# Attention-stage projections as 256-column groups that share one PSUM bank

## The chip, the cores and the metric

The kernel runs on one core of a Trainium2 chip. The metric is the device time of one launch in microseconds. All times below are of that kind or come from one profiled execution of the kernel before.

## The reference

A transformer layer with pre-LayerNorm: attention with 32 heads over a sliding window of 256 positions, and then a feed-forward network with SiLU, each with its residual. Inputs are bf16.

```python
B, S, D = 1, 2048, 1024;  H = 32; Dh = 32; W = 256;  F = 3584
qkv = _layernorm(x) @ wqkv                    # q, k, v per head
scores = einsum("bhqd,bhkd->bhqk", q, k) * Dh**-0.5
mask = (i - j >= 0) & (i - j < W)
o = softmax(where(mask, scores, -1e9)) @ v
h = x + o.reshape(B, S, D) @ wo
h2 = h + silu(_layernorm(h) @ w1) @ w2
```

## The kernel before

The 2,048 tokens are four blocks of 512 (`NB` = 4), and the model dimension is eight tiles of 128 (`KT` = 8). The order of instructions on every engine is the order of the code (the tile framework's manual schedule); the framework adds the semaphore waits that the accesses call for.

The projections are built from groups: eight matmuls of 128x128 weights with 512 moving columns, accumulated in one bank of PSUM, then one copy by VectorE (`dve`) into SBUF. `v_group` (L235 to L242) makes 128 tokens by 512 columns of v, `qk_group` (L244 to L252) makes 128 columns of q or k for the 512 tokens of a block, and `wo_group` (L266 to L276) makes 128 tokens by 512 columns of the output projection, which VectorE adds to the residual (L273) and a late DMA stores to `h_dram`. The bank comes from `next_acc` (L231), which goes through `acc_banks` in turn; in the attention stages these are the two banks `acc0` and `acc1`. [...]these two, two for attention's outputs (`o_ps`), and four for scores (`sc`).

There are four attention stages, each of 24 groups. In stages one to three the dense work is the v, q and k projection of blocks 1, 2 and 3, and in stage four the output projection of blocks 0 to 2. Woven into each is the attention of the block before. An object `Stream` (L415) holds this as a list of bursts (the score matmuls of four or eight heads, followed by exponentials on ScalarE and by masks on GpSimd) and a list of pieces (the products of the probabilities with v in `attn_out`, L377, and for each 8 of them a reciprocal and a multiplication on VectorE, `attn_norm`, L392). Before each matmul of a group, `between(kt)` is called, 192 times a stage. By two conditions on its count (L435 and L438) it issues a burst or a piece so that they are spread evenly; the first stage has 16 of each and the others 20. TensorE's instructions thus stand as: a few dense matmuls, a burst or a piece, a few dense matmuls, and so on.

After each group the stage takes one step from a list `steps`: the LayerNorm of a later block, on VectorE. A statistics step (`ln_stats`, L176) has two `bn_stats` of 512 columns and one aggregation; four further steps find the reciprocal root (`rstd_steps`, L184), and four scale a tile (`ln_norm`, L201). When the steps are done, `turns` issue DMA transposes. In stage three (block 3) no steps are left; in stage four they are the second LayerNorm of block 0, taken from n = 12 on, two for each group from n = 16.

Work on VectorE is done in program order, so a copy out of PSUM stands behind the steps and attention norms issued before it. Before the four stages lie the projections of block 0, and after them the feed-forward network, with six banks in `acc_banks`; those use `v_group`, `qk_group` and `wo_group` as they are.

Of the kernel before, what the change touches and what calls it, by code (L numbers as in the profile page):

```python
# [9 lines left out]
F32 = mybir.dt.float32  # L10
I32 = mybir.dt.int32
ACT = mybir.ActivationFunctionType
ALU = mybir.AluOpType

P = 128
# [29 lines left out]
def kernel(  # L45
# [10 lines left out]
    nc = tc.nc  # L56
# [3 lines left out]
    S, D = x2d.shape  # L60
    F = B_w1.shape[1]
    H = N_HEADS
    DH = D // H
    assert DH == 32 and D == 1024 and S == 2048 and F == 3584
    KT = D // P
    FT = F // P
    NB = S // 512
    G = H // 4
# [4 lines left out]
    small = ctx.enter_context(tc.tile_pool(name="small", bufs=2))  # L73
# [5 lines left out]
    h_dram = dram.tile([S, D], BF16, name="h_dram")  # L79
# [26 lines left out]
    wqk = view(r_w, 0, KT, 2 * D)  # L106
    wv = view(r_w, 16384, KT, D)
    w1 = view(r_w, 0, KT, F)
    lnT_b = [view(r_w, 24576, KT, 512), view(r_t, 0, KT, 512)]
    x_ring = [view(r_o, i * 1024, 1024) for i in range(8)]  # L110
    wo = view(r_o, 0, KT, D)
    t_in = [view(r_t, i * 1024, 1024) for i in range(2)]
    r_in = [view(r_a, 16384, 1024), view(r_a, 17408, 1024), *t_in, view(r_a, 22528, 1024), view(r_a, 23552, 1024)]
    t_out = [view(r_t, 2048 + i * 1024, 1024) for i in range(2)]
    qT = [view(r_a, (4096, 8192, 12288, 0)[b], G, 512) for b in range(NB)]
    kT = [view(r_a, 16384 + 4096 * b, G, 512) for b in range(NB)]
    v = view(r_a, 32768, S // P, H, VW)
# [55 lines left out]
    def ln_half(xt, stats, c):  # L173
        nc.vector.bn_stats(out=stats[:, c, :], in_=xt[:, c * 512:(c + 1) * 512])

    def ln_stats(xt, st, j, half_done=None):  # L176
        stats = half_done
        if stats is None:
            stats = small.tile([P, 2, 6], F32, name="ln_st", tag="ln_st")
            ln_half(xt, stats, 0)  # L180
        ln_half(xt, stats, 1)
        nc.vector.bn_aggr(out=st[:, j, :], in_=stats[:])
# [46 lines left out]
    acc_banks = list(a[:] for a in acc_ps)  # L229

    def next_acc():  # L231
        acc_n[0] += 1
        return acc_banks[acc_n[0] % len(acc_banks)]

    def v_group(b, j, c, copy, between=None):  # L235
        acc = next_acc()
        for kt in range(KT):
            if between:
                between(kt)
            nc.tensor.matmul(acc, lhsT=lnT_b[b % 2][:, kt, j * P:(j + 1) * P], rhs=wv[:, kt, c * 512:(c + 1) * 512],  # L240
                             start=(kt == 0), stop=(kt == KT - 1))
        copy(out=v[:, b * 4 + j, c * 16:(c + 1) * 16, 0:DH], in_=acc.rearrange("p (h d) -> p h d", d=DH))  # L242

    def qk_group(b, which, g, copy, between=None):  # L244
        acc = next_acc()
        col0 = which * D + g * P
        for kt in range(KT):
            if between:
                between(kt)
            nc.tensor.matmul(acc, lhsT=wqk[:, kt, col0:col0 + P], rhs=lnT_b[b % 2][:, kt, :],  # L250
                             start=(kt == 0), stop=(kt == KT - 1))
        copy(out=(qT, kT)[which][b][:, g, :], in_=acc)  # L252
# [7 lines left out]
    late = []  # L260

    def run_late():
        while late:
            late.pop(0)()

    def wo_group(b, j, c, between=None):  # L266
        acc = next_acc()
        for g in range(G):
            if between:
                between(g)  # L270
            nc.tensor.matmul(acc, lhsT=qT[b][:, g, j * P:(j + 1) * P], rhs=wo[:, g, c * 512:(c + 1) * 512],  # L271
                             start=(g == 0), stop=(g == G - 1))
        nc.vector.tensor_tensor(out=t_out[j % 2][:, c * 512:(c + 1) * 512], in0=acc,  # L273
                                in1=r_in[(b * 4 + j) % 6][:, c * 512:(c + 1) * 512], op=ALU.add)
        if c == 1:
            late.append(lambda: nc.sync.dma_start(out=h_dram[(b * 4 + j) * P:(b * 4 + j + 1) * P, :], in_=t_out[j % 2]))  # L276
# [138 lines left out]
    class Stream:  # L415
# [18 lines left out]
        def between(self, kt):  # L434
            if self.seen * self.n >= self.done * 192:  # L435
                self.bursts[self.done]()
                self.done += 1
            if self.seen * self.n * 2 >= (self.given * 2 + 1) * 192:  # L438
                if pending:
                    pending.pop(0)()  # L440
                coming.append(self.pieces[self.given])
                if len(coming) > self.behind:
                    pending.append(coming.pop(0))
                self.given += 1
            self.seen += 1

    dve, act = nc.vector.tensor_copy, nc.scalar.copy


    st, rs = ln_tiles("a")  # L450
# [99 lines left out]
    for j in range(4):  # L550
        load_x(1, j)

    def ln1_steps(b):
        st, rs = ln_tiles("a")
        xs = [x_ring[(b % 2) * 4 + j] for j in range(4)]
        steps = [lambda j=j: ln_stats(xs[j], st, j) for j in range(4)]
        steps += rstd_steps(st, rs)
        for j in range(4):
            steps.append(lambda j=j: ln_norm(xs[j], st, rs, j))
        return steps, [lambda j=j: ln_transpose(xs[j], lnT_b[b % 2], j) for j in range(4)]  # L560

    def ln2_steps(b):
        st, rs = ln_tiles("b")
        hb = h_blk[b]
        load = lambda: nc.sync.dma_start(out=hb, in_=h_dram[b * 512:(b + 1) * 512, :].rearrange("(j p) d -> p j d", p=P))
        steps = [load]
        steps += [lambda j=j: ln_stats(hb[:, j, :], st, j) for j in range(4)]
        steps += rstd_steps(st, rs)
        for j in range(4):
            steps.append(lambda j=j: ln_norm(hb[:, j, :], st, rs, j))  # L570
        turns = [lambda j=j: ln_transpose(hb[:, j, :], ln2T[b], j) for j in range(4)]
        return steps[:-2] + [turns[0], steps[-2], turns[1], steps[-1]] + turns[2:]

    steps = sum(ln1_steps(1), [])
    for g0 in range(0, G, 4):
        for w in range(2):
            for g in range(g0, g0 + 4):
                qk_group(0, w, g, dve if g % 2 else act)
                n = g0 * 2 + w * 4 + g % 4
# [5 lines left out]
    def load_w1(kt):  # L585
        nc.sync.dma_start(out=w1[:, kt, :], in_=w1_v[:, kt, :])
# [4 lines left out]
    steps, turns = ln1_steps(2)  # L591
    pending, coming = [], []
    stream = Stream(0)
    dense = [lambda j=j, c=c: v_group(1, j, c, dve, stream.between) for j in range(4) for c in range(2)]
    dense += [lambda w=w, g=g: qk_group(1, w, g, dve, stream.between) for g in range(G) for w in range(2)]
    for n in range(24):
        run_late()
        dense[n]()
        if steps and n >= 1 and n != 3:
            steps.pop(0)()  # L600
        elif turns and n % 3 == 2:
            turns.pop(0)()
# [2 lines left out]

    for b in range(2, NB):
        stream = Stream(b - 1)
        dense = [lambda j=j, c=c: v_group(b, j, c, dve, stream.between) for j in range(4) for c in range(2)]
        dense += [lambda w=w, g=g: qk_group(b, w, g, dve, stream.between) for g in range(G) for w in range(2)]
        if b + 1 < NB:  # L610
            for j in range(4):
                load_x(b + 1, j)
            steps, turns = ln1_steps(b + 1)
        else:
            steps, turns = [], []
            nc.sync.dma_start(out=wo[:, 0:4, :], in_=wo_v[:, 0:4, :])
            nc.sync.dma_start(out=wo[:, 4:8, :], in_=wo_v[:, 4:8, :])
            load_res(0)
            load_res(1)
        for n in range(24):  # L620
            run_late()
            if b == NB - 1 and n in (4, 10, 14):
                load_w1({4: 7, 10: 6, 14: 5}[n])
            dense[n]()
            if steps and n >= 1 and n != 3:
                steps.pop(0)()
            elif turns and n % 3 == 2:
                turns.pop(0)()
        assert not steps and not turns


    dense = []
# [6 lines left out]
    steps = []  # L639
    stream = Stream(NB - 1)  # L640
    for n in range(24):
        run_late()
        if n % 2 == 0 and n >= 2 and n // 2 + 5 < S // P:
            load_res(n // 2 + 5)
        wo_group(*dense[n], stream.between)
        if n in (1, 4, 7, 12, 15):
            load_w1((1, 4, 7, 12, 15).index(n))
        if n == 9:
            steps = ln2_steps(0)
            steps.pop(0)()  # L650
        if n == 17:
            nc.sync.dma_start(out=w2[0], in_=w2_v[:, 0:4, :])
        for _ in range(1 if n < 16 else 2):
            if steps and n >= 12:
                steps.pop(0)()
# [29 lines left out]
    for b in range(NB):  # L685
# [4 lines left out]
        for ft in range(FT):  # L690
            acc = h1_group(b, ft)
# [7 lines left out]
            if b == 0 and 6 <= ft < 14:  # L699
                j, c = divmod(ft - 6, 2)  # L700
# [4 lines left out]
        steps = ln2_steps(b + 1) if b + 1 < NB else []  # L705
# [5 lines left out]
        for j in range(4):  # L711
# [9 lines left out]
            for acc, (c0, c1) in zip(accs, cols):  # L721
                mm2(acc, j, c0, c1, early, FT)
                nc.vector.scalar_tensor_tensor(out=t_out[j % 2][:, c0:c1], in0=acc[:, 0:c1 - c0], scalar=0.5,  # L723
                                               in1=t_in[j % 2][:, c0:c1], op0=ALU.mult, op1=ALU.add)
# [36 lines left out]
```

## Time and profile before

| what | value |
|---|---|
| time, median of 3 runs | 691.38 us (691.37 to 691.72) |
| the profiled execution, its own time | 691.51 us |
| its span, first to last instruction | 689.8 us |
| granted TensorE clock, mean | 1.000 |
| start and projections of block 0 | 0 to 49.4 us |
| the four attention stages | 49.4 to 285.2 us |
| the feed-forward network | 285.2 to 689.8 us |
| HBM | 70 GB/s over the span |

The page gives, for each engine, the time in which it was busy and its share of the span; the chain that ended last is followed back from the last instruction to what released each. PE stands for TensorE's matmuls, PEld for its weight loads, DVE for VectorE, ACT for ScalarE and POOL for GpSimd. A group line has the source line, the engine, the operation, the names written and read, shapes and count, then busy time, mean length in ns, and the engine's idle time just before these instructions with what ended it. Matmuls are pipelined: a 512-column matmul is shown with 379 ns while the next one starts 216 ns after it. Some matmul records are missing from the trace, a few in a hundred.

### The profile page before, as it was taken

The page shows a single profiled execution, that of the slowest core. Times are in us where ns is not written, and L with a number is a line of the kernel's source. Part 1 is how long each engine was busy: PE and PEld are TensorE (multiplying, and loading weights), DVE is VectorE, ACT ScalarE, POOL GpSimd, SP SyncE. Part 2 cuts the span into 40 slices and gives each one's busy share as a digit, 9 for nine tenths or more (in the row PEclk, how much of TensorE's full clock was granted, in tenths as well). Part 3 has the DMA queues.
Part 4 walks back from the last instruction along what each step waited for, and adds up shares of the span by engine and source line. Part 5 has one row for each costly group of instructions (what it writes and reads, how often), then busy time and mean ns, then how long its engine had stood idle before and what let it go on. Part 6 is the DMA issues. An engine that isn't in the chain of part 4 may idle for free.

```text
span 689.8 us, 14125 instructions
## 1 busy us (share of the span) xinstructions
PE 676.4 (98%) x5895; PEld 331.6 (48%) x6011; DVE 290.0 (42%) x613; ACT 244.7 (35%) x464; POOL 160.6 (23%) x295
## 2 busy tenths in 40 slices
PE   9999999999999999999999999999999999999998
PEld 4444555555555555544444444444444444444445
DVE  5267646744444449534316133343133251333111
ACT  7326666676666667421310033300133100233000
POOL 1007666566666656500000000000000000000000
PEclk9999999999999999999999999999999999999999
DMA  7842342136341889871023310022200023100110
GB/s 258 275 63 70 48 97 38 25 63 184 73 131 18 251 226 298 207 267 60 2 85 114 85 39 0 1 91 70 85 0 1 27 88 92 38 1 1 30 39 24
DMA packets 78640, 61.48 MB, mean 89 GB/s; under 512 B 52464, under 2 KB 62704, under 8 KB 78576
## 3 DMA queue, kind: packets, MB, share of 16 engines
q1 hardware_dynamic: 77888, 59.78, 31.0%
q8 instruction: 47, 0.77, 0.5%
q10 hardware_dynamic: 688, 0.79, 0.3%
q14 instruction: 17, 0.14, 0.1%
HBM read 39.85 MB, written 8.39 MB: 70 GB/s over the span
## 4 chain that ended last, share of the span: by engine, by line
PE 97%; issue 1%; DMA 0%; DVE 0%; DVEq 0%
PE hacc L671 19%; PE hacc L708 17%; PE acc L250 16%; PE acc L708 10%; PE acc L671 9%; PE acc L240 7%; PE acc L271 7%; PE o_ps L383 5%; PE sc L303 3%; PE hacc L271 1%; PE sc L355 1%; PE o_ps L240 1%; PE sc L329 1%; DMA r_o<-in_A_x_dram 0%; PE tp L218 0%
## 5 line engine op out<-in xcount | busy, mean ns | idle before, releaser
L373 POOL TENSOR_SCALAR_AFFINE_SELECT r_e<-r_e 128x512 bf16<-128x512 bf16 (+1 forms) x288 | 157.6, 562 | 124.9 <-ACT r_e L363 61.2
L708 PEld LDWEIGHTS <-r_a 128*128 128x128 bf16 x952 | 90.9, 98 | 103.0
L671 PEld LDWEIGHTS <-r_w 128*128 128x128 bf16 x896 | 87.4, 98 | 105.0
L708 PE MATMUL hacc<-r_a 128*128 128x512 bf16 (+2 forms) x607 | 121.8, 359 | 0.5
L671 PE MATMUL hacc<-r_e,r_w 128*128 128x512 bf16 x444 | 99.7, 379 | 0.5
L315 ACT ACTIVATE r_e<-sc 128x768 bf16<-128x768 f32 x96 | 78.3, 816 | 48.1 <-PE sc L303 48.1
L680 ACT ACTIVATE r_n<-hacc 128x512 f32<-128x512 f32 x30 | 17.9, 598 | 178.9 <-PE hacc L671 175.5
L708 PE MATMUL acc<-r_a 128*128 128x512 bf16 x329 | 73.5, 379 | 0.4
L250 PEld LDWEIGHTS <-r_w 128*128 128x128 bf16 x512 | 44.2, 97 | 46.2 <-issue 1.0
L250 PE MATMUL acc<-r_t,r_w 128*128 128x512 bf16 x233 | 60.3, 379 | 2.4 <-issue 1.7
L252 DVE CAST r_a<-acc 128x512 bf16<-128x512 f32 x56 | 38.6, 690 | 55.4 <-PE acc L250 42.3
L250 PE MATMUL acc<-r_w 128*128 128x512 bf16 x240 | 58.0, 379 | 1.5 <-issue 1.0
L383 PEld LDWEIGHTS <-r_e 128*128 128x128 bf16 x1440 | 47.4, 96 | 17.9
L271 PE MATMUL acc<-r_o,r_a 128*128 128x512 bf16 x188 | 49.5, 379 | 1.9 <-issue 1.3
L671 PE MATMUL acc<-r_e,r_w 128*128 128x512 bf16 x213 | 48.9, 379 | 0.3
L383 PE MATMUL o_ps<-r_a,r_e 128*128 128x33 bf16 x1440 | 48.1, 178 | 0.1
L316 ACT ACTIVATE r_e<-sc 128x256 bf16<-128x256 f32 x96 | 37.8, 394 | 0.0
L723 DVE SCALAR_TENSOR_TENSOR r_t<-hacc,r_t 128x512 bf16<-128x512 f32 (+2 forms) x22 | 14.0, 635 | 56.4 <-PE hacc L708 55.1
L723 DVE SCALAR_TENSOR_TENSOR r_t<-acc,r_t 128x512 bf16<-128x512 f32 x12 | 8.3, 692 | 64.2 <-PE acc L708 58.8
L681 DVE SCALAR_TENSOR_TENSOR r_a<-r_n,hacc 128x512 bf16<-128x512 f32 x30 | 20.6, 688 | 33.0 <-ACT r_n L680 33.0
L671 PE MATMUL hacc<-r_a,r_w 128*128 128x512 bf16 x139 | 32.6, 379 | 0.3
L271 PEld LDWEIGHTS <-r_a 128*128 128x128 bf16 x256 | 21.8, 97 | 22.3
(100 smaller groups left out, 538.6 us busy)
## 6 DMA issues: line engine op xcount, KB each, us to landing
r_w<-in_B_w_dram SPq DMA_DIRECT2D x8, 896.0 KB, 5.0
r_a<-in_B_w_dram SPq DMA_DIRECT2D x7, 1024.0 KB, 7.3
r_w<-in_A_wqkv_dram SPq DMA_DIRECT2D x4, 1024.0 KB, 8.0
h_dram<-r_t SPq DMA_DIRECT2D x16, 256.0 KB, 2.5
r_t<-h_dram SPq DMA_DIRECT2D x16, 256.0 KB, 2.8
out_dram<-r_t SPq DMA_DIRECT2D x31, 128.0 KB, 1.7
r_o<-in_A_x_dram SPq DMA_DIRECT2D x15, 256.0 KB, 4.9
r_e<-h_dram SPq DMA_DIRECT2D x3, 1024.0 KB, 5.7
```

What stands on the lines that cost most here:

```text
L240: nc.tensor.matmul(acc, lhsT=lnT_b[b % 2][:, kt, j * P:(j + 1) * P], rhs=wv[:, kt, c * 512:(c + 1) * 512], start=(kt == 0), stop=(kt == KT ...
L250: nc.tensor.matmul(acc, lhsT=wqk[:, kt, col0:col0 + P], rhs=lnT_b[b % 2][:, kt, :], start=(kt == 0), stop=(kt == KT - 1))
L252: copy(out=(qT, kT)[which][b][:, g, :], in_=acc)
L271: nc.tensor.matmul(acc, lhsT=qT[b][:, g, j * P:(j + 1) * P], rhs=wo[:, g, c * 512:(c + 1) * 512], start=(g == 0), stop=(g == G - 1))
L303: nc.tensor.matmul(sc[hh // 2][half * 64:half * 64 + 64, hh % 2, col:col + qb - qa], lhsT=kT[t // 4][r0:r0 + DH, g, k0:k0 + 64], rhs=qT[b] ...
L315: nc.scalar.activation(out=tri[:, :, :, 64:256], in_=both, func=ACT.Exp, scale=scale)
L316: nc.scalar.activation(out=e[:, 1024:1280].rearrange("p (h q) -> p h q", q=P), in_=bank[:, :, 192:320], func=ACT.Exp, scale=scale)
L373: nc.gpsimd.affine_select(out=dst, in_=src, pattern=[[0, n] for n in dst.shape[1:-1]] + [[sgn, P]], compare_op=ALU.is_ge if upper else ALU ...
L383: nc.tensor.matmul(o_ps[pair][:, qt * 2 + hh, 0:VW], lhsT=chunk_of(i, bank, piece, pair, hh), rhs=v[:, b * 4 + kt, g * 4 + pair * 2 + hh, ...
L671: nc.tensor.matmul(acc, lhsT=w1[:, kt, ft * P:(ft + 1) * P], rhs=ln2T[b][:, kt, :], start=(kt == 0), stop=(kt == KT - 1))
L708: nc.tensor.matmul(acc[:, 0:c1 - c0], lhsT=gT[:, ft, j * P:(j + 1) * P], rhs=w2[ft // 4][:, ft % 4, c0:c1], start=(ft == 0), stop=(ft == F ...
L723: nc.vector.scalar_tensor_tensor(out=t_out[j % 2][:, c0:c1], in0=acc[:, 0:c1 - c0], scalar=0.5, in1=t_in[j % 2][:, c0:c1], op0=ALU.mult, o ...
```

## The change

The groups of the four stages are made by new functions `v_half`, `qk_half` and `wo_half`. All three go through `half_groups`, which makes the 512 columns in two halves of 256, one after the other: eight matmuls with 256 moving columns, then the copy (or the addition) of those 256 columns. Both halves of every group lie in the first bank, `acc_banks[0]`, at columns 0 to 255 and 256 to 511; the second bank isn't used in these stages. `between` is called at every second matmul, so four times in a half and 192 times in a stage as before. Weights are loaded once for each half.

The LayerNorm steps are cut finer: `stat_steps` splits a statistics step in two (the first `bn_stats`; the second and the aggregation). A list `fine` can hold one step, which is issued behind the copy of the first half; from n = 2 (in stage four from n = 12) one step a group goes there, and the step behind the group stays. The LayerNorm of block 1, ahead of the first stage, keeps its unsplit steps.

```diff
+    def half_groups(between, mm, out):
+
+        for h in range(2):
+            acc = acc_banks[0][:, h * 256:(h + 1) * 256]
+            for kt in range(KT):
+                if kt % 2 == 0:
+                    between(kt)
+                mm(acc, kt, h * 256, kt == 0, kt == KT - 1)
+            out(acc, h * 256)
+            if h == 0 and fine:
+                fine.pop(0)()
+
+    fine = []
...
+    def qk_half(b, which, g, between):
+        col0 = which * D + g * P
+
+        def mm(acc, kt, n0, start, stop):
+            nc.tensor.matmul(acc, lhsT=wqk[:, kt, col0:col0 + P], rhs=lnT_b[b % 2][:, kt, n0:n0 + 256], start=start, stop=stop)
+
+        half_groups(between, mm, lambda acc, n0: dve(out=(qT, kT)[which][b][:, g, n0:n0 + 256], in_=acc))
...
+    def stat_steps(xs, st, split):
+        if not split:
+            return [lambda j=j: ln_stats(xs[j], st, j) for j in range(4)]
+        steps = []
+        for j in range(4):
+            stats = small.tile([P, 2, 6], F32, name="ln_st", tag="ln_st")
+            steps += [lambda j=j, s=stats: ln_half(xs[j], s, 0), lambda j=j, s=stats: ln_stats(xs[j], st, j, s)]
+        return steps
...
-        dense = [lambda j=j, c=c: v_group(b, j, c, dve, stream.between) for j in range(4) for c in range(2)]
-        dense += [lambda w=w, g=g: qk_group(b, w, g, dve, stream.between) for g in range(G) for w in range(2)]
+        dense = [lambda j=j, c=c: v_half(b, j, c, stream.between) for j in range(4) for c in range(2)]
+        dense += [lambda w=w, g=g: qk_half(b, w, g, stream.between) for g in range(G) for w in range(2)]
...
+            if n >= 2 and len(steps) > 1:
+                fine.append(steps.pop(0))
             dense[n]()
             if steps and n >= 1 and n != 3:
                 steps.pop(0)()
...
+        if n >= 12 and steps:
+            fine.append(steps.pop(0))
-        wo_group(*dense[n], stream.between)
+        wo_half(*dense[n], stream.between)
```

More of the change, by code (lines that the diff above doesn't have):

```diff
@@ L233, in next_acc, with v_half, out, mm @@
         return acc_banks[acc_n[0] % len(acc_banks)]
+    def half_groups(between, mm, out):
[9 more added lines that the diff above has]
+    fine = []
+    def v_half(b, j, c, between):
+        def mm(acc, kt, n0, start, stop):
+            nc.tensor.matmul(acc, lhsT=lnT_b[b % 2][:, kt, j * P:(j + 1) * P], rhs=wv[:, kt, c * 512 + n0:c * 512 + n0 + 256], start=start, stop=stop)
+        def out(acc, n0):
+            h0 = c * 16 + n0 // DH
+            dve(out=v[:, b * 4 + j, h0:h0 + 8, 0:DH], in_=acc.rearrange("p (h d) -> p h d", d=DH))
+        half_groups(between, mm, out)
+    def qk_half(b, which, g, between):
+        col0 = which * D + g * P
+        def mm(acc, kt, n0, start, stop):
+            nc.tensor.matmul(acc, lhsT=wqk[:, kt, col0:col0 + P], rhs=lnT_b[b % 2][:, kt, n0:n0 + 256], start=start, stop=stop)
+        half_groups(between, mm, lambda acc, n0: dve(out=(qT, kT)[which][b][:, g, n0:n0 + 256], in_=acc))
+    def wo_half(b, j, c, between):
+        def mm(acc, g, n0, start, stop):
+            nc.tensor.matmul(acc, lhsT=qT[b][:, g, j * P:(j + 1) * P], rhs=wo[:, g, c * 512 + n0:c * 512 + n0 + 256], start=start, stop=stop)
+        def out(acc, n0):
+            n0 += c * 512
+            nc.vector.tensor_tensor(out=t_out[j % 2][:, n0:n0 + 256], in0=acc, in1=r_in[(b * 4 + j) % 6][:, n0:n0 + 256], op=ALU.add)
+        half_groups(between, mm, out)
+        if c == 1:
+            late.append(lambda: nc.sync.dma_start(out=h_dram[(b * 4 + j) * P:(b * 4 + j + 1) * P, :], in_=t_out[j % 2]))
     def v_group(b, j, c, copy, between=None):
@@ L551, with ln1_steps @@
         load_x(1, j)
-    def ln1_steps(b):
+    def stat_steps(xs, st, split):
[6 more added lines that the diff above has]
+        return steps
+    def ln1_steps(b, split=True):
         st, rs = ln_tiles("a")
         xs = [x_ring[(b % 2) * 4 + j] for j in range(4)]
-        steps = [lambda j=j: ln_stats(xs[j], st, j) for j in range(4)]
+        steps = stat_steps(xs, st, split)
         steps += rstd_steps(st, rs)
@@ L566, in ln2_steps @@
         steps = [load]
-        steps += [lambda j=j: ln_stats(hb[:, j, :], st, j) for j in range(4)]
+        steps += stat_steps([hb[:, j, :] for j in range(4)], st, True)
         steps += rstd_steps(st, rs)
@@ L572, in ln2_steps @@
         return steps[:-2] + [turns[0], steps[-2], turns[1], steps[-1]] + turns[2:]
-    steps = sum(ln1_steps(1), [])
+    steps = sum(ln1_steps(1, False), [])
     for g0 in range(0, G, 4):
@@ L593 @@
     stream = Stream(0)
-    dense = [lambda j=j, c=c: v_group(1, j, c, dve, stream.between) for j in range(4) for c in range(2)]
-    dense += [lambda w=w, g=g: qk_group(1, w, g, dve, stream.between) for g in range(G) for w in range(2)]
+    dense = [lambda j=j, c=c: v_half(1, j, c, stream.between) for j in range(4) for c in range(2)]
+    dense += [lambda w=w, g=g: qk_half(1, w, g, stream.between) for g in range(G) for w in range(2)]
     for n in range(24):
         run_late()
+        if n >= 2 and len(steps) > 1:
+            fine.append(steps.pop(0))
         dense[n]()
@@ L623 @@
                 load_w1({4: 7, 10: 6, 14: 5}[n])
+            if n >= 2 and len(steps) > 1:
+                fine.append(steps.pop(0))
             dense[n]()
@@ L644 @@
             load_res(n // 2 + 5)
-        wo_group(*dense[n], stream.between)
+        if n >= 12 and steps:
+            fine.append(steps.pop(0))
+        wo_half(*dense[n], stream.between)
         if n in (1, 4, 7, 12, 15):
```

## The prediction

> **What bounds the kernel now.** I read the page first (busy shares, then the chain that ended last), then the table of stages, then the groups by form, and last single stretches of the timeline for the latencies. The page:
>
> ```profile
> PE 676.4 (98%) x5895; PEld 331.6 (48%) x6011; DVE 290.0 (42%) x613; ACT 244.7 (35%) x464; POOL 160.6 (23%) x295
> ...
> PE 97%; issue 1%; DMA 0%; DVE 0%; DVEq 0%
> ```
>
> TensorE is busy 98% of the span and is 97% of the chain; no engine that it waits for has a share to speak of. So whatever is added to TensorE's stream in these stages, work or waiting, comes out at the end nearly one for one, and a gain on another engine is worth nothing. The change touches four stages: the projections of blocks 1, 2 and 3, and the output projection of blocks 0 to 2, each woven with attention. I cut the span at their borders, which the chain shows (columns: stretch, length, busy time and instructions of PE, PEld, DVE, ACT, POOL, then clock and DMA):
>
> ```profile
> 49.40:104.60 55.20, 53.67 (x765) 27.58 (x764) 33.67 (x81) 35.17 (x96) 37.50 (x96) 1.00 0.35 82
> 104.60:166.40 61.80, 59.88 (x1021) 32.93 (x1034) 37.57 (x85) 42.23 (x74) 40.03 (x64) 1.00 0.27 57
> 166.40:226.70 60.30, 58.40 (x1010) 32.21 (x1027) 25.98 (x56) 40.89 (x73) 39.90 (x64) 1.00 0.39 100
> 226.70:285.20 58.50, 56.65 (x975) 31.24 (x990) 35.09 (x83) 39.52 (x71) 39.25 (x63) 1.00 0.92 253
> ```
>
> In each, TensorE is full and VectorE, ScalarE and GpSimd have a third or more of the time free. The groups by form give the pieces:
>
> ```profile
> L250 PE MATMUL acc<-r_t,r_w 128*128 128x512 bf16 x233 | 60.3, 379 | 2.4 <-issue 1.7
> ...
> L252 DVE CAST r_a<-acc 128x512 bf16<-128x512 f32 x56 | 38.6, 690 | 55.4 <-PE acc L250 42.3 <-PE sc L303 12.6
> ...
> L395 DVE TENSOR_TENSOR r_n<-o_ps,recip 128x256 bf16<-128x256 f32 x64 | 27.2, 425 | 2.2
> ...
> L174 DVE BATCH_NORM_STATS2 ln_st<-r_o 128x6 f32<-128x512 bf16 x28 | 17.8, 678 | 0.0
> ...
> L708 PE MATMUL hacc<-r_a 128*128 128x256 bf16 x28 | 3.2, 272 | 0.1
> ```
>
> The eviction of a 512-column group takes VectorE 690 ns and VectorE waits for TensorE before it, not the other way round. The idle time ahead of L250 is in part missing records: gaps of 53 ns are two matmul steps of 216 less 379. That two banks hide the copy is seen here:
>
> ```profile
> 172.04 0.69 DVE L242 CAST r_a<-acc 128x512 bf16<-128x512 f32 x1 [1.38 <-PE acc L240]
> ...
> 172.20 0.77 PEld L240 LDWEIGHTS <-r_t 128*128 128x128 bf16 x5
> 172.23 1.24 PE L240 MATMUL acc<-r_w,r_t 128*128 128x512 bf16 x5
> ```
>
> The cast runs from 172.04 to 172.73, and the next group's matmuls start at 172.23 beside it, in the other bank.
>
> **What the Trainium skill says.** "PSUM — Partial Sum Buffer", section "PSUM bank collisions raise a hardware error": TensorE writing a bank while VectorE reads the same bank and the same 32 partitions is an error, at disjoint columns too, and the chip doesn't hold either back; the program has to. No stretch of this trace shows two engines at one bank, so the trace neither confirms nor denies it. "Perfetto Trace Analysis", section "Optimizing Tensor Performance", says groups should rotate through banks so that an eviction overlaps the next group: the stretch above agrees (0.69 us hidden). "TensorE: Matmul & The Clock Gate", "Back-to-back issue gap": 518 cycles for 512 columns and 262 for 256. The trace agrees with both, in the chain and in the last token tile, which already has a 256-column group:
>
> ```profile
> 295.05 3.45 PE acc L671 x16
> ```
> ```profile
> 680.79:683.85 3.06, 3.06 (x28) 1.00 0.13 46
> ```
>
> That is 3.45/16 = 0.216 us a matmul at 512 columns and 3.06/28 = 0.109 us at 256, with one weight load (98 ns, hidden) for each.
>
> **The change, part by part.** Each of 24 groups in four stages becomes two halves of eight 256-column matmuls: 192 halves, 1,536 matmuls in place of 768.
>
> 1. Steps of the matmuls. 1,536 x 0.1092 = 167.7 us against 768 x 0.2158 = 165.7: +2.0 us on TensorE. The 768 more weight loads lie under the matmuls, as they do in the 256-column stretch above.
>
> 2. The wait for the bank. All halves use the same bank. If the skill's rule holds, the first matmul of each half waits until the cast of the half before has ended, and that cast until the half's last matmul has ended. Nothing of the two overlaps any more. The price from three stretches: the end of a 256-column group,
>
> ```profile
> 683.52 0.49 PE L708 MATMUL hacc<-r_a 128*128 128x256 bf16 x3
> ```
> ```profile
> 684.05 0.42 DVE L723 SCALAR_TENSOR_TENSOR r_t<-hacc,r_t 128x256 bf16<-128x256 f32 x1 [2.36 <-PE hacc L708]
> ```
>
> three matmuls from 683.52 to 684.01, the last begun at 683.74 (two steps of 0.109 later), VectorE from 684.05: 0.31 us from the last start to the eviction, which takes 0.425 us for 256 columns (this row, and L395's mean). For the way back to TensorE, the one idle wait for VectorE early in the kernel:
>
> ```profile
> 4.95 0.60 DVE L468 TENSOR_SCALAR r_e<-r_o,mean 128x256 bf16<-128x256 bf16 x2
> ...
> 5.36 0.40 PE L218 MATMUL tp<-ident,r_e 128*128 128x128 bf16 x2 [0.28 <-DVE r_e L468]
> ```
>
> Of the pair from 4.95 the first ended at about 5.29 (0.342 us each by L468's group), and the matmul that needs it begins some 0.055 us later. So from the last matmul's start to the next half's first: 0.309 + 0.425 + 0.055 = 0.789 us, where it would have been 0.109. A stall of 0.68 us, if TensorE has nothing else there. Times 192: 130.6 us.
>
> 3. What covers it. TensorE runs in program order, so only what stands between two halves helps: a burst of scores or a piece of attention called at kt = 0. `between` is now called at every second kt, four times a half, still 192 times a stage. Counting its two conditions through: in the first stage (16 bursts, 16 pieces) all 16 bursts fall at kt = 0 and all pieces at kt = 4. In the other three (20 and 20), 8 bursts and 8 pieces fall at kt = 0. From the starts in the timeline a burst costs TensorE 0.43 to 0.46 us and a piece 0.38, 0.46 or 0.60. Cover: 16 x 0.455 = 7.3 us in the first stage; in each other 4 x (0.43 + 0.46 + 0.38 + 0.60) = 7.5 us, 22.5 in all. 130.6 - 29.8 = 100.8 us.
>
> 4. VectorE's queue. What is queued ahead of a cast now delays TensorE directly. From one cast's end to the next's readiness there are some 1.1 us (eight steps of 0.109 and 0.31, less the 0.055). The LayerNorm steps fit: the change cuts a statistics step of 1.57 us (2 x 0.68 + 0.21) into 0.68 and 0.89, one behind each half, and the norm is 0.63 (rows L174, L182, L202). The attention norms (0.20 + 0.425) come late in a half: one whose piece is called at kt = 4 ends about 0.2 us after the cast could have begun, one at kt = 6 with its norm in the middle likewise 0.19. First stage 16 x 0.2 = 3.2; the others 4 x 0.2 + 4 x 0.19 = 1.6 each, 4.8. In the last stage two steps follow the second half once n reaches 16, which overruns by some 0.7 us three times: 2. Sum 10.0 us. Bounds: 0 if the norms slip in ahead, 25 if most halves with a piece lose 0.2 to 0.3.
>
> 5. Shorter LayerNorm chains: the steps end sooner and the transposes are issued about three groups earlier. The instructions and the transfers are the same ones, only earlier on SyncE's queue, and TensorE waits for none of them before: worth 0.
>
> Sum: 2.0 + 100.8 + 10.0 = 112.8 us. The profiled execution took 691.51 (span 689.8 and 1.7 around it), 0.13 above the median; 691.5 + 112.8 = 804. ScalarE (42) and GpSimd (40) keep their work in stages of some 87 us, so neither becomes the bound.
>
> Bounds of the stall: if the weight load too sits behind the wait, up to 98 ns (the load's row) more for each half, +13 us for the 128 that nothing covers, at most some +17; if VectorE takes up the cast 60 ns sooner when it sits waiting, -12 us. I take 0.68, since in these groups the trace has the waits on the MATMUL instructions (64 of L250) and hardly on the loads (4).
>
> **Rivals.**
> - The halves are not held apart (disjoint columns count as independent). For: the casts are short and a half's columns are wanted again a whole half later (0.87 us against the 0.68 the cast needs, so covered). Against: the skill's rule. Then only step 1 and a few late casts count: 2 to 9 us, 693.5 to 700.
> - The clock falls. The same skill page's first part says a full idle window of about 3.4 us halves the clock. For: TensorE would stand idle some 30% of these stages. Against: each stall is 0.7 us, and the granted clock is 1.00 in every slice before. If it came, 1,536 x 0.109 = +168 us on top: about 970.
> - Not slower: the 7 us of idle ahead of L240, L250 and L271 (the group rows) are real waits for queue and eviction, and shorter evictions take them away. Then -7 + 2 = 686.5. It decides only if what the shared bank costs is under (7 - 2)/192 = 26 ns a half. Against: the gaps of 53 and 159 ns fit missing records.
>
> **How the numbers follow.** Held apart by bank: 0.87, 804, own range 780 to 838 (the bounds: -10 and -12 below, with 2 for the cover; +15 and +17 above). Not held apart 0.07; clock falls 0.04; not slower 0.02. The range is the likeliest's own, as the others hold 0.13. What the measurement can tell is about 0.2%, 1.4 us: faster 0.02; the second case's lower end touches no change, so 0.03; slower 0.95.
>
> **What would show it.** PE's idle ahead of the new matmul line should be about 100 us in total over 170 waits, released by the new casts of 128x256 at 425 ns; stages of 82 to 90 us instead of 55 to 62; the stretch after the last stage unchanged at 405 us; clock 1.00. Matmul steps of 0.109 show step 1. It is wrong if PE starts a half while the cast of the one before runs, or if the waits mean far from 0.6 us.

## The result and the profile after

The changed kernel takes 800.15 us (median of 4 runs, 799.88 to 800.51) against 691.55 for the kernel before on the same chip: a ratio of 1.157, interval 1.1553 to 1.1588. Its profiled execution took 800.51 us, with a span of 798.8. The spans differ by 109.0 us.

The page's first line for the kernel after shows where the change sits (busy time and share of the span by engine):

```profile
PE 713.0 (89%) x6779; PEld 410.3 (51%) x6779; DVE 304.1 (38%) x709; ACT 244.2 (31%) x464; POOL 160.6 (20%) x295
```

TensorE is no longer full. Part of its larger busy sum is a matter of display: a matmul that ends before a wait is shown with its whole length, and matmul records that were missing before are there now. The table of stages of the kernel after, cut at the first dense matmul of each stage and of the feed-forward network (columns as before: stretch, length, then busy time and count by engine, clock, DMA):

```profile
50.55:133.07 82.52, 61.64 (x957) 47.27 (x957) 37.78 (x104) 34.77 (x97) 37.27 (x96) 1.00 0.22 57
133.07:220.04 86.97, 66.94 (x1204) 51.56 (x1204) 39.50 (x108) 40.80 (x73) 40.40 (x64) 1.00 0.19 52
220.04:306.70 86.66, 67.24 (x1217) 51.95 (x1217) 29.58 (x80) 40.80 (x73) 39.83 (x64) 1.00 0.17 50
306.70:394.04 87.34, 66.81 (x1201) 51.71 (x1201) 39.37 (x107) 40.71 (x72) 39.71 (x64) 1.00 0.62 177
394.04:798.80 404.76, 402.10 (x1962) 185.92 (x1959) 133.78 (x243) 66.87 (x112) 0.41 (x1) 1.00 0.18 56
```

Cut in the same way, the stages before took 55.18, 60.26, 60.29 and 59.86 us. So the increases are 27.3, 26.7, 26.4 and 27.5 us, 107.9 in all, and the other 1.1 us lies ahead of the first stage. Of that, 0.4 is a wait that is taken up below; the rest is within what the start varies from run to run (stage one begins at 49.8 to 51.0 us in the runs with halves whose banks are two tiles). The feed-forward network takes 404.8 us in both. No engine took over: ScalarE and GpSimd did the same work in more time. What TensorE waits for is in the list of waits of its matmuls (total us, times, longest):

```profile
PE acc L263 <- DVE r_a L265: 37.3, 81, 0.6
PE acc L269 <- DVE r_t L273: 20.0, 40, 0.9
PE acc L251 <- DVE r_a L255: 19.7, 42, 0.9
```

L251, L263 and L269 are the matmuls of the three new functions, and L255, L265 and L273 their copies. These three rows hold 163 waits for the copy of the half before, and smaller rows, where one function follows another, 6 more: 169 of the 191 halves that follow a half. Of the other 22, 11 wait 0.14 us, and 11 have a longer piece of attention ahead of them that fills the time. Every one of the 191 begins at least 0.785 us after the last matmul of the half before began. The 77 us of the three rows are only what stands after a matmul's modelled end, 0.163 us later than the moment at which the next matmul would have begun in a stream. One half in stage two:

```profile
155.07 1.03 PE L251 MATMUL acc<-r_w 128*128 128x256 bf16 x8 [0.18 <-DVE r_a L255]
...
156.14 0.43 DVE L255 CAST r_a<-acc 128x256 bf16<-128x256 f32 x1 [0.28 <-PE acc L251]
...
156.62 0.38 PE L251 MATMUL acc<-r_w 128*128 128x256 bf16 x2 [0.52 <-DVE r_a L255]
```

Eight matmuls begin at 155.07, the last at 155.83; the cast runs from 156.14, and the next half begins at 156.62, 0.79 us after the last matmul began. Over all halves in the trace, the last start to the copy takes 0.310 us wherever VectorE is free, the copy 0.41 to 0.43, and copy's end to the next matmul 0.053.

### The profile page after: what moved, and what is told of

Its sections match the earlier page's. It is cut to its first block, busy times and chain, and to the rows that moved or that the text cites. A ratio compares the mean times of both kernels' runs of the same rounds, so it can differ in the third digit from the quotient of the medians.

```text
span 798.8 us, 15870 instructions
## 1 busy us (share of the span) xinstructions
PE 713.0 (89%) x6779; PEld 410.3 (51%) x6779; DVE 304.1 (38%) x709; ACT 244.2 (31%) x464; POOL 160.6 (20%) x295
## 4 chain that ended last, share of the span: by engine, by line
PE 56%; DVE 3%; issue 1%; DMA 0%
PE hacc L730 16%; PE hacc L767 15%; PE acc L767 9%; PE acc L730 8%; PE acc L269 5%; DVE r_t L273 2%; PE hacc L315 1%; PE o_ps L427 1%; PE sc L347 0%; PE acc L315 0%; DMA h_dram<-r_t 0%; DVE r_n L439 0%; DVE recip L438 0%; DVE rs_b L197 0%; DVE ln_t L196 0%
## 5 line engine op out<-in xcount | busy, mean ns | idle before, releaser
L767 PEld LDWEIGHTS <-r_a 128*128 128x128 bf16 x952 | 90.9, 98 | 103.0
L730 PEld LDWEIGHTS <-r_w 128*128 128x128 bf16 x896 | 87.5, 98 | 104.8
L263 PEld LDWEIGHTS <-r_w 128*128 128x128 bf16 x768 | 71.1, 97 | 61.0 <-issue 50.0
L263 PE MATMUL acc<-r_t,r_w 128*128 128x256 bf16 x512 | 70.4, 271 | 27.1 <-DVE r_a L265 25.6
L269 PE MATMUL acc<-r_o,r_a 128*128 128x256 bf16 x384 | 53.6, 272 | 20.7 <-DVE r_t L273 20.0
L265 DVE CAST r_a<-acc 128x256 bf16<-128x256 f32 x96 | 40.5, 422 | 81.0 <-PE acc L263 81.0
L269 PEld LDWEIGHTS <-r_a 128*128 128x128 bf16 x384 | 35.3, 97 | 31.3 <-issue 26.1
L263 PE MATMUL acc<-r_w 128*128 128x256 bf16 x256 | 35.6, 272 | 12.8 <-DVE r_a L265 11.8
L251 PE MATMUL acc<-r_w,r_t 128*128 128x256 bf16 x256 | 35.0, 272 | 13.4 <-DVE r_a L255 12.7
L251 PEld LDWEIGHTS <-r_t 128*128 128x128 bf16 x256 | 23.8, 97 | 20.5 <-issue 16.5
L407 ACT ACTIVATE r_e<-sc 128x512 bf16<-128x512 f32 x32 | 19.4, 608 | 46.3 <-PE sc L399 46.3
```

Source lines behind the costliest of these rows:

```text
L265: half_groups(between, mm, lambda acc, n0: dve(out=(qT, kT)[which][b][:, g, n0:n0 + 256], in_=acc))
L407: nc.scalar.activation(out=e[:, :, 0:256], in_=sc[pair][:, :, 0:256], func=ACT.Exp, scale=scale)
L730: nc.tensor.matmul(acc, lhsT=w1[:, kt, ft * P:(ft + 1) * P], rhs=ln2T[b][:, kt, :], start=(kt == 0), stop=(kt == KT - 1))
L767: nc.tensor.matmul(acc[:, 0:c1 - c0], lhsT=gT[:, ft, j * P:(j + 1) * P], rhs=w2[ft // 4][:, ft % 4, c0:c1], start=(ft == 0), stop=(ft == F ...
```

## The experiments

**The second half in the other bank.** Nothing else is touched.

```diff
-            acc = acc_banks[0][:, h * 256:(h + 1) * 256]
+            acc = acc_banks[h][:, 0:256]
```

> The changed kernel with the second half of each group in the other bank; halves, weight loads, split LayerNorm steps and the order of everything stay. Theory A (the shared bank makes each half wait for the copy of the half before): nearly all of the 108.6 us goes, and what is left is the step of the smaller matmuls, 2.0 us, with perhaps 1 us of late copies: 693.5 to 695. TensorE's waits for the copies, 81 us of idle time in the groups, fall under 3 us. Rival B (the halves themselves cost it: twice the weight loads, twice the copies, steps in between): it stays above 780.

Measured: 698.98 us (before beside it 691.58; ratio 1.0108, 1.0089 to 1.0127). 101 of the 108.6 us go. Halving as such is not the cost, and rival B falls. But the time lies above the expected 693.5 to 695: 5 us are left over, and TensorE's waits for copies are not under 3 us. This is the one large row that is left, all of it in stage four; it is taken up further down.

```profile
PE acc L269 <- DVE r_t L273: 4.5, 4, 1.8
```

**Whole groups in one bank.** The kernel before, with the bank fixed.

```diff
-        acc = next_acc()
+        acc = acc_banks[0] if between else next_acc()
```

> The kernel before, with its 512-column groups of the four stages all in the first bank; nothing is halved and no step is split. Theory A: 96 waits of 0.416 (last matmul's start to copy) + 0.692 (copy) + 0.053 (back) - 0.216 = 0.945 us make 90.7; bursts and pieces at a group's start cover 3.6 us in the first stage and 3.3 in each other, 13.5; late attention norms add some 3: +80 us, 772. Rival B: as nothing is halved, no change, 691.5.

Measured: 772.10 us (ratio 1.1159, 1.1141 to 1.1178), where the sum gave 772. Its waits, in the same view:

```profile
PE acc L250 <- DVE r_a L252: 30.9, 45, 0.9
PE acc L271 <- DVE r_t L273: 16.1, 23, 0.9
PE acc L240 <- DVE r_a L242: 15.5, 21, 1.1
```

Half as many waits, each longer by what the 512-column copy and matmul are longer: the price by parts holds at another size. Halves in one bank (800) are worse than whole groups in one bank (772), since by the sums 192 waits of 0.68 us cost more than 96 of 0.945.

**Bursts and pieces gathered at the half's start.** The same instructions, with the score bursts and attention pieces moved into the waits.

```diff
-                if kt % 2 == 0:
+                for _ in range(4 if kt == 0 else 0):
                     between(kt)
```

> The changed kernel, with all four calls for bursts and pieces of a half made ahead of its first matmul in place of every second one. The waits stay; only what lies in them changes. Theory A with its sum for the cover: 32 of 48 half starts have a burst or a piece in the first stage, 40 of 48 in the others, together 14.6 + 3 x 18.8 = 71.0 us of cover against 29.8, and the late attention norms go (4 us): 800 - 45 = 755. Rival C (bursts and pieces themselves wait for something that comes late, so TensorE stands still all the same): 795 to 800. Rival B: 800, since TensorE's work is the same.

Measured: 756.00 us (ratio 1.093, 1.0914 to 1.0946), where the sum for the cover gave 755. The waits from a half's last matmul to the next half's first are as long as ever, 0.79 us in 181 of 191, but more of that time has work in it. Rival C falls.

**Both: whole groups in one bank, gathered.** All eight calls of a group ahead of its first matmul.

> 512-column groups in one bank (772.1), with all eight calls for bursts and pieces of a group made ahead of its first matmul. Theory A: 24 waits of 0.945 us a stage; bursts and pieces at the group starts cover 14.6 us of 22.7 in the first stage and 4 x 4.58 = 18.3 in each other: 8.1 + 3 x 4.4 = 21 us are left, with 2 for late copies: 712 to 716. If the cover saturates or the burst's own inputs come late: 730 or more.

Measured: 713.97 us (ratio 1.0323, 1.0309 to 1.0338), inside the 712 to 716. With one bank, 22 us over the kernel before, this is the best one-bank form tried; it gives back 86 of the 108.6 us.

**One tile over two banks.** As the first experiment, but the two banks are one tile.

```diff
-    acc_ps = [ps.tile([P, 512], F32, name=f"acc{i}") for i in range(2)]
+    acc_both = ps.tile([P, 2, 512], F32, name="acc")
+    acc_ps = [acc_both[:, i, :] for i in range(2)]
...
-            acc = acc_banks[0][:, h * 256:(h + 1) * 256]
+            acc = acc_banks[h][:, 0:256]
```

> As the run with the second half in the other bank, but both banks belong to one tile of 128 x 2 x 512. If the wait is a matter of the bank: 693.5 to 695, as there. If it comes from two accesses to one tile, whatever the bank: 800.

Measured: 852.37 us (ratio 1.2322, 1.2303 to 1.2340). Both numbers were wrong: it is 52 us slower even than the changed kernel. The 800 was the nearer one: the four stages take what they take in the changed kernel (343.9 us against 343.5), and the 52 us lie in front of them and behind. The waits of this kernel, whose lines stand one later in the stages (L731 and L741 are the feed-forward network's first matmul and its copy):

```profile
PE acc L264 <- DVE r_a L266: 37.3, 81, 0.6
PE acc L731 <- DVE r_a L741: 21.1, 15, 1.4
PE acc L270 <- DVE r_t L274: 19.8, 40, 0.9
PE acc L252 <- DVE r_a L256: 19.6, 42, 0.9
PE acc L295 <- DVE r_a L297: 5.9, 7, 0.9
```

The main waits of the stages are the same to 0.2 us as in the changed kernel, though successive halves lie in different banks. And places outside the stages that go through the banks in turn, the projections of block 0 (L295) and the feed-forward network, now wait too.

**The kernel before with one tile.** Only the two lines of the tile, in the kernel before.

> The kernel before, whole groups in turn over two banks, with one edit: the two banks belong to one tile. In the run with halves and one tile the four stages took what they take in the changed kernel, though the halves lay in two banks, and the other stages took 52 us more. If the wait follows the tile: the four stages lose what whole groups in one bank lost, 80 us, and the others 52: about 824. If it was something of the halves' columns in a common tile: 691.5.

Measured: 824.33 us (ratio 1.1915, 1.1891 to 1.1939). Its four stages take 315.7 us, as in the run with whole groups in one bank (315.8). So TensorE's writes and VectorE's reads of one PSUM tile are put in order in this program whatever bank or columns they touch, and this order is enough to make the wait in the changed kernel. Two separate tiles within one bank were not tried, so whether a shared bank alone would make it too stays open. In the waits of this run, L251 and L253 are the q and k groups:

```profile
PE acc L251 <- DVE r_a L253: 36.9, 52, 0.9
PE acc L672 <- DVE r_a L682: 21.1, 15, 1.4
PE acc L272 <- DVE r_t L274: 16.0, 23, 0.9
```

**The finer LayerNorm steps alone.** The kernel before with `stat_steps` and two steps behind a group.

```diff
-        dense[n]()
+        if n >= 2 and len(steps) > 1:
+            fine.append(steps.pop(0))
+        dense[n]()
+        while fine:
+            fine.pop(0)()
```

> The kernel before (512-column groups, two banks) with the finer LayerNorm steps alone: statistics steps split in two, two steps behind a group from n = 2 on, transposes issued about three groups earlier. Theory A: VectorE's queue covers nothing here, no change: 691.0 to 692.0. Rival D (the earlier LayerNorm chain is worth something, or costs it): more than 1.4 us off either way.

Measured: 691.84 us against 691.67 (ratio 1.0004, 0.9996 to 1.0012): no difference.

**The changed kernel without the finer steps.** `stat_steps` gives whole steps and `fine` stays empty.

> The changed kernel without the finer steps: statistics steps of 1.57 us whole, one step behind the second half of each group as before. Theory A: between two copies VectorE has about 1.1 us, so each of the 12 whole statistics steps makes the next copy some 0.45 us late, +5 us, less what the double steps cost at the end of stage four (2 us): 803 to 806. If VectorE's queue doesn't matter: 799 to 801.

Measured: 802.78 us (ratio 1.1611, 1.1595 to 1.1627), 2.6 over the changed kernel and just under the range. Stages one and two, with four whole statistics steps each, are 0.67 and 0.83 us longer than in the changed kernel: 0.19 us a step, where 0.45 were expected. Stage three, which has no steps, is the same, and stage four is 0.66 longer, with whole steps but without the double ones; the other 0.4 us lie ahead of stage one. VectorE's queue matters, by less than I had reckoned.

**Where the 5 us of the first experiment lie.** Its stages take 55.64, 60.72, 60.78 and 66.02 us: the first three 0.46 to 0.49 over before, as the matmul steps say, and stage four 6.2. I first took this for the three LayerNorm steps that stand in a group there from n = 16, and took the extra one out.

> The kernel with the second half in the other bank took 699.0, 5 us over what the matmul steps explain, and its trace has TensorE waiting 4.5 us for late copies in stage four, where three LayerNorm steps stand behind each group from n = 16. Here stage four takes one step a group up to n = 15 and two from 16, as before the change. If VectorE's queue there is the 5 us: 693.5 to 695. If something else of the halves costs it: 698 to 699.

Measured: 699.70 us (ratio 1.0124, 1.0107 to 1.0142). Next I put back the groups of stage four.

> Halves over two banks in stages one to three, stage four with its 512-column groups and steps as before. In the trace of the run with halves over two banks everywhere, stages one to three are 0.46 to 0.48 us longer each than before, as the smaller matmuls' step says, and stage four is 6.2 us longer. If all that is over comes from stage four: 1.5 us for the steps and up to 0.4 for the first hand-over, 693.0 to 693.6. If the stages are longer for a reason that follows the halves: 696 or more.

Measured: 699.68 us (ratio 1.0125, 1.0108 to 1.0141). Both miss, for a reason in my edits. They left the second LayerNorm's statistics steps split, so its chain was four steps longer with no place to run in. In the timeline and waits of the second of the two runs:

```profile
285.39 4.00 SPq L206 DMA_TRANSPOSE r_a<-r_a  x3
```
```profile
PE acc L728 <- issue: 3.9, 1, 3.9
```

The last three transposes that the feed-forward network needs are issued from 285.39, where before they were issued from 277.06, and its first matmul (L728) stands 3.9 us. With those steps whole, and stage four thus as before:

> Halves over two banks in stages one to three, and stage four wholly as before, its second LayerNorm's statistics steps whole too. In the run that left these split (699.7), the four steps more made the chain one that ended behind the stage: its last transposes were issued at 285.4, 8 us later than before, and TensorE stood 4.25 us ahead of the feed-forward network. If that is all: 1.5 us for the matmul steps and 0.4 for the first hand-over are left, 693.0 to 693.6, and no gap over 1 us ahead of the feed-forward network. If the halves cost something else: 696 or more.

Measured: 694.28 us (ratio 1.0040, 1.0026 to 1.0054), a little above the 693.6. Its stages take 55.64, 60.72, 61.03 and 59.84: the fourth is as before, and the first three are 0.46, 0.46 and 0.74 longer (the third ends with a hand-over to stage four, whose first whole group has a wait of 0.2 us for the copy of the last half); 0.75 us lie ahead of the first stage. With 2.8 us over before, no large cost of the halves is left.

The other way, halves over two banks in all stages, with a third output tile in stage four (`t_3`, the third at columns 33792 to 34816 of `r_a`, which that stage doesn't use):

```diff
-            nc.vector.tensor_tensor(out=t_out[j % 2][:, n0:n0 + 256], in0=acc, ...
+            nc.vector.tensor_tensor(out=t_3[(b * 4 + j) % 3][:, n0:n0 + 256], in0=acc, ...
```

> Halves over two banks everywhere, with a third output tile in stage four, so that an addition of the output projection waits for the store of three token tiles ago instead of two. With two tiles VectorE stood waiting for a store 3.3 and 2.4 us at two places, and TensorE behind it 1.7 each. If that wait is most of the 6.2 us in stage four: 694 to 696, with no wait of L273 for a DMA left. If it is the queue of LayerNorm steps: 699.

Measured: 695.98 us (ratio 1.0062, 1.0049 to 1.0075). Stage four falls from 66.02 to 62.25 us, and no addition waits for a store any more. What went is this, in the timeline of the first experiment:

```profile
254.15 0.57 SPq L277 DMA_DIRECT2D h_dram<-r_t  x1
...
260.87 0.42 DVE L273 TENSOR_TENSOR r_t<-acc,r_a 128x256 bf16<-128x256 f32 x1 [3.32 <-DMA h_dram<-r_t]
```

VectorE stands 3.3 us behind the store of two token tiles ago (issued at 254.15, landed at 260.79, in a stage whose DMA engines were 92% busy before the change too), and the half behind it on TensorE 1.7 us. It stands so a second time at 289.49, for 2.4 us. With halves the first addition into a tile comes half a group earlier than before, and the store no longer has landed. Why the store takes 6.6 us here, and 2.0 to 4.8 in the kernel before, was not tried. Stage four is still 2.4 us over before. 0.5 are the matmul steps; the rest goes with three waits for late additions that the first experiment has too, shown with 0.57, 0.45 and 0.52 us. The first two stand behind LayerNorm steps in VectorE's queue, so my first guess held for about 1.3 us of the 6.2; the third is the feed-forward network's first matmul.

## Why the prediction was right, point by point

The forecast was 804 and the result 800.15; the sum was 112.8 us over before, and 108.6 were measured.

- **Step 1, the matmul steps, 2.0 us**: the run with halves over two banks has 0.46 to 0.49 us a stage over before where nothing else is in the way, and 0.5 were reckoned. Right.
- **Step 2, the wait at each half**: its parts were 0.309, 0.425 and 0.055, and the trace shows 0.310, 0.41 to 0.43 and 0.053. Each part is right to 0.015 us (there are 191 such waits between halves and not 192, worth 0.7 us), and the price carried over to whole groups (772 for 772). The reason given for it was the bank. What the runs show is another: the wait comes with the tile, for one tile over two banks waits just as much. In the changed kernel the halves share both, so the same 804 follows from either; it is luck that the forecast didn't depend on which of the two it named. "PSUM — Partial Sum Buffer", section "PSUM bank collisions raise a hardware error", would require it for a shared bank in any case; no run here has two engines at one bank unordered, so that part was not tried.
- **Step 3, the cover, 29.8 us**: the waits between halves sum to 136.1 us in the trace (start to start, less a matmul's step). With the 2.0 us of step 1 that makes 138.1; the stages grew by 107.9, so 30.2 us were covered. Right, also directly: with halves over two banks, in stages one to three, where TensorE doesn't wait, the same hand-overs take 7.1 to 7.5 us a stage for their bursts and pieces. And moving the work into the waits bought 44 us where 45 were reckoned.
- **Step 4, VectorE's queue, 10.0 us**: this is the term that was mis-sized. In the trace 43 copies begin later than 0.31 us after the last matmul's start, by 6.8 us in all: 2.0, 1.3, 1.1 and 2.5 us in the four stages, where 3.2, 1.6, 1.6 and 3.6 were reckoned. The late attention norms are there, at the places counted: in stage one, 14 of the 16 pieces at kt = 4 make a copy late, but by 0.14 us each and not 0.2; in stages two and three eight each, by 0.12 to 0.14, with one of 0.35. In stage four 12 copies are late by 0.06 to 0.17 us, and one by 1.0, behind double steps (reckoned at 2) whose products are slow there, as the last section shows. A stretch of the changed kernel shows a part of why less is lost:

```profile
153.98 0.19 DVE L438 RECIPROCAL recip<-o_ps 128x8 f32<-128x8 f32 x1
154.20 0.42 DVE L439 TENSOR_TENSOR r_n<-o_ps,recip 128x256 bf16<-128x256 f32 x1
...
154.59 0.43 DVE L255 CAST r_a<-acc 128x256 bf16<-128x256 f32 x1
154.93 0.68 DVE L174 BATCH_NORM_STATS2 ln_st<-r_o 128x6 f32<-128x512 bf16 x1
```

The cast begins 0.03 us before the norm is shown to end, and the statistics begin 0.09 us before the cast's end. Adding up the lengths shown makes the queue too long, here by 0.03 to 0.09 us at each such place; the whole of the difference is not accounted for.
- **Step 5**, earlier LayerNorm chains, 0: right (691.84 against 691.67).
- **Not in the sum**: 0.4 us at the start of stage one, where the first half waits for the last copy of block 0's projections.
- **The rivals**: a half doesn't start while the copy of the one before runs, so the case in which disjoint columns count as independent didn't occur; the clock was 1.00 throughout in spite of 169 stalls; and the idle time that the last rival would have won back was not real. In the run of 694.28 us, no matmul record is missing, TensorE shows 59.84 us busy of the 59.84 of stage four, and that stage is as long as before.

## What to carry to other kernels

Where one engine fills the span, ask first whether an edit lets its stream overlap the evictions (the copies out of PSUM) as before. Here a second buffer was worth the whole round trip (last start to copy, copy, way back), less one matmul step, at every turn that no other work covered: 0.68 us at 256 columns and 0.945 at 512. Smaller groups in one buffer made it worse, as there were more turns. In this program the buffers had to be separate tiles, not columns or banks of one tile. If only one can be spared, keep the groups large and put the independent work of the busy engine into the turns: here that is 714 instead of 800 us.

## What the runs showed of the hardware that was not expected

**Some small operations of VectorE took two to four times as long beside GpSimd.** In the changed kernel, stage four, with GpSimd's masks on the second line:

```profile
368.90 0.16 DVE L196 TENSOR_TENSOR ln_t<-ln_t,rs_b 128x4 f32<-128x4 f32 x1
369.06 2.64 POOL L417 TENSOR_SCALAR_AFFINE_SELECT r_e<-r_e 128x512 bf16<-128x512 bf16 x4 [2.10 <-ACT r_e L359]
...
369.93 0.48 DVE L196 TENSOR_TENSOR ln_t<-ln_t,rs_b 128x4 f32<-128x4 f32 x1
370.45 0.55 DVE L197 SCALAR_TENSOR_TENSOR rs_b<-ln_t,rs_b 128x4 f32<-128x4 f32 x1
```

In this trace the same product of 128x4 (L196) takes 0.16 us in all 17 places where GpSimd is at rest or only begins, and 0.35 to 0.59 in the four where GpSimd runs. Of the five norms of 128x1024 (L202) beside GpSimd two take 0.73 and 0.82 us, and three 0.54, as without it; L195 and L197 differ from place to place in the same way. Casts out of PSUM (0.42) and the statistics (0.68) don't change. "SBUF — State Buffer", section "Who interferes with whom", has VectorE's second SBUF input shared with GpSimd, which fits the products with two inputs, but not the places that are unchanged; that this is the cause was not tried.

**In the traces, the clock fell after a single long stand, and not with many short ones.** In the run with halves in stages one to three that stood 3.9 us ahead of the feed-forward network (columns: stretch, length, PE busy and count, granted clock, DMA share, GB/s):

```profile
291.10:292.10 1.00, 0.97 (x5) 1.00 0.44 143
292.10:293.10 1.00, 1.00 (x5) 0.60 0.89 188
293.10:294.10 1.00, 1.00 (x18) 0.50 0.90 238
294.10:295.10 1.00, 0.78 (x3) 0.50 1.04 387
295.10:296.10 1.00, 1.00 (x5) 0.70 0.87 338
296.10:297.10 1.00, 1.00 (x22) 1.00 0.13 51
```

The clock was 0.50 for 3.4 us, begun when matmuls already ran again. It fell for as long in the run with 2.5 us of idle at that place, and not in the traced execution of the one with two stands of 1.7 us, nor in any trace with stalls of 0.7 alone. That this is a rule is not shown: one untraced execution of the first experiment (700.99 us) and one of the changed kernel without the finer steps (804.68 us) have a mean clock of 0.998 too, and they took 1.5 to 3 us more than the others of their kind.
